# Loading the second half of w2 in even pieces instead of three uneven ones, and the first MLP bias in five transfers instead of two

## The chip, the cores and the metric

The kernel runs on one core of a Trainium2 chip. The metric is the device time of one execution in microseconds (us). The kernel before takes 134.59 us (median of 7 runs, 134.49 to 134.99).

## The reference

One decode step for two sequences (B = 2) with width D = 576. A layer norm of `x` feeds two branches whose sum is added to `x`. All inputs are bf16.

```python
xn = layernorm(x)                                    # 2 x 576
# branch A: attention over the last W = 2048 of 8192 cached positions
q = (xn @ wq)                                        # 32 query heads of 128, 16 key/value heads
p = softmax(q . k_cache[:, :, Sk - W:, :] * 128**-0.5)
a = (p . v_cache[:, :, Sk - W:, :]) @ wo             # 4096 -> 576
# branch B: MLP with squared ReLU
h = relu(xn @ w1 + b1) ** 2                          # 576 -> 4608
b = h @ w2 + b2                                      # 4608 -> 576
out = x + a + b
```

Nearly all the work is reading: 16 tiles of 2 MB of keys and values, and the weights wq (4.7 MB), w1 (5.3 MB), wo (4.7 MB) and w2 (5.3 MB); 53.6 MB in all, each byte used once.

## The kernel before, in words

**Tiling of the attention.** The key and value caches are cut into NU = 8 units (four heads of one sequence each). `load_k(u)` and `load_v(u)` (line 106) each issue one transfer of 2 MB, 128 rows of 16384 bytes, one row per partition. `step(u)` transposes the keys of unit u on TensorE, forms its scores and softmax, and in between does the value product of unit u - 2. `issue_flat` (line 119) loads wq, w1 and wo, in this order of time, into the one buffer `wbig`, each as one transfer; so w1 waits until wq has been read by the matmuls, and wo until w1 has.

**The queues.** All large loads are issued from the queue of SP, in the order of the program. The few small ones (x, the two rows of four of b1 at line 417, b2 at line 418, and the output) are issued from the queue of ACT. Every transfer, on either queue, has one of eight completion semaphores, which are handed out in turn; a transfer that gets a semaphore for a second time is issued only when the transfer that had it before has landed, unless an earlier wait of the same queue already showed that. The order of the hand-outs is that of the compiled program. In the kernel before it is: x, k0, b1 (first), b1 (second), b2, wq, k1, v0 on the eight semaphores; then k2 on that of x, v1 on that of k0, k3 on that of the first half of b1, v2 on that of the second, and so on. At the end, the three pieces of `w2x_sb` are on the semaphores of k7, v6 and v7, and the last piece of `w2c_sb` on that of wo.

**The end.** `out_ps` is one PSUM tile in which 128 columns of attention output (wo, 32 rows of four matmuls), the first half of the MLP (w2a, 18 rows) and its second half (18 rows) are added up by `out_acc`, four matmuls for each row of a partition. w2 is seen as two halves; in each a partition holds 18 consecutive rows of 576 values, 1152 bytes each. The first half is one transfer (`w2a_sb`, 20736 bytes per partition). The second half comes in pieces, in this order on the SP queue:

- `w2b_sb`: rows 0 to 8 of each partition (10368 bytes per partition)
- `w2c_sb`: rows 9 to 13 (5760 bytes), then rows 14 and 15 (2304 bytes)
- `w2x_sb`: row 17, in three transfers of 85, 25 and 18 partitions (`XS`, line 77; lines 442 to 444)
- `w2c_sb`: row 16 (1152 bytes)

The matmuls follow in the order of arrival (lines 451 to 457); row 17 (`w2x_sb`) is taken just before row 16, which is the last. ACT then copies `out_ps` to SBUF (line 460) and stores it (line 461).

Of the kernel before, what the change touches and what calls it, by code (L numbers as in the profile page):

```python
# [8 lines left out]
F32 = mybir.dt.float32  # L9
BF16 = mybir.dt.bfloat16  # L10
# [6 lines left out]
def kernel(  # L17
# [14 lines left out]
    nc = tc.nc  # L32
    P = 128
    B, Sq, D = A_x.shape
# [26 lines left out]
    NG4 = 4  # L61
# [11 lines left out]
    WC = Dh // WR  # L73
    FR = L1 // P
    assert HW == 32 * FR and QH * 2 == NC and NC * WC == 32
    W2P = [(0, 9), (9, 14), (14, 16), (16, 17)]
    XS = [(0, 85), (85, 110), (110, 128)]
    BS = 16
    MB = BS * (B - 1) + 1
    RM = 32 * (NG4 - 1) + MB  # L80
# [3 lines left out]
    const = ctx.enter_context(tc.tile_pool(name="const", bufs=1))  # L84
    kvpool = ctx.enter_context(tc.tile_pool(name="kvpool", bufs=6))
    wbig = ctx.enter_context(tc.tile_pool(name="wbig", bufs=1))
    w2pool = ctx.enter_context(tc.tile_pool(name="w2pool", bufs=1))
# [5 lines left out]
    def matmul(*a, **k):  # L93
        tc.keep_in_program_order(nc.tensor.matmul(*a, **k))  # L94
# [24 lines left out]
        nc.sync.dma_start(out=tl[:, 0:n], in_=w.rearrange("r n -> (r n)").rearrange("(p l) -> p l", p=P))  # L119
        return tl  # L120

    const.tile([P, 112], F32, name="pad_0")
    w2x_sb = const.tile([P, D], BF16, name="w2x_sb")
    xb_sb = const.tile([B + 1, D], BF16, name="xb_sb")
    x_sb = xb_sb[0:B, :]
    nc.scalar.dma_start(out=x_sb, in_=x2d)
# [54 lines left out]
    for t0, half, k0, n, pc in ((0, 0, 0, NK, 0), (0, 1, 0, NK, 1), (1, 0, 1, NK - 1, 1), (1, 1, 0, NK - 1, 0)):  # L181
# [11 lines left out]
                          in_=own[:].unsqueeze(2).to_broadcast([P, NC, WC]))  # L193
# [11 lines left out]
                          in_=ident[0:2 * NG4, 0:2 * NG4].rearrange("p (x g) -> p x g", g=NG4).unsqueeze(3)  # L205
                          .to_broadcast([2 * NG4, 2, NG4, B]))

    b1_sb = const.tile([2 * NG4, HW], BF16, name="b1_sb")
    w2_rows = B_w2.rearrange("(x p r) n -> x p (r n)", x=2, r=FR)


    out_ps = psum.tile([RM, OQ], F32, tag="out", name="out_ps")
    nc.vector.memset(out_ps[:], 0.0)

    def out_acc(lhsT, rhs, o, start=False, stop=False):
        for i in range(4):
            matmul(out_ps[32 * i:32 * i + MB, :], lhsT=lhsT, rhs=rhs[:, o * D + i * OQ:o * D + (i + 1) * OQ],
                   start=start, stop=stop, skip_group_check=True, tile_position=(0, 32 * i))
# [91 lines left out]
    hT_sb = const.tile([P, 2, FR, MB], BF16, name="hT_sb")  # L310
# [75 lines left out]
    def step(u):  # L386
        fin = None
        w = u - 2
        with_pv = w >= 0
        for g in range(NG):  # L390
            transposes(u, g)
            if with_pv and g == 1:
                pv(w, 0, 2)
            if with_pv and g == 2:
                pv(w, 1, 2)
                fin = pv_end(w)
            if g == TG + 1:
                scores(u, 0)
            if g == TG + 2 and fin:
                fin()  # L400
        scores(u, 1)
        softmax(u)
# [10 lines left out]
    softmax(0)  # L413
    load_v(2)
    b1_rows = B_b1.rearrange("(x n) -> x n", n=HW)
    for i in range(0, 2 * NG4, 4):
        nc.scalar.dma_start(out=b1_sb[i:i + 4, :], in_=b1_rows[i:i + 4, :])
    nc.scalar.dma_start(out=xb_sb[B:B + 1, :], in_=B_b2.rearrange("(o n) -> o n", o=1))
    step(1)
    load_k(4)  # L420
# [12 lines left out]
    mlp_h(w1_sb)  # L433
    wo_sb = issue_flat(A_wo, "wo")
    w2a_sb = w2pool.tile([P, FR * D], BF16, name="w2a")
    r9 = W2P[0][1]
    w2b_sb = kvpool.tile([P, r9 * D], BF16, tag="kv", name="w2b")
    w2c_sb = w2pool.tile([P, (FR - 1 - r9) * D], BF16, name="w2c")
    nc.sync.dma_start(out=w2a_sb[:], in_=w2_rows[0])
    nc.sync.dma_start(out=w2b_sb[:], in_=w2_rows[1, :, 0:r9 * D])  # L440
    for r0, r1 in W2P[1:]:
        if r1 == FR - 1:
            for p0, p1 in XS:
                nc.sync.dma_start(out=w2x_sb[p0:p1, :], in_=w2_rows[1, p0:p1, (FR - 1) * D:FR * D])
        nc.sync.dma_start(out=w2c_sb[:, (r0 - r9) * D:(r1 - r9) * D], in_=w2_rows[1, :, r0 * D:r1 * D])
    step(NU - 1)
    pv_all(NU - 2)
    pv_all(NU - 1)
# [1 line left out]
        out_acc(ws[:, r, :], wo_sb, r)  # L450
    for r in range(FR):
        out_acc(hT_sb[:, 0, r, :], w2a_sb, r)
    for r in range(FR - 1):
        if r == FR - 2:
            out_acc(hT_sb[:, 1, FR - 1, :], w2x_sb, 0)
        w, o = (w2b_sb, r) if r < r9 else (w2c_sb, r - r9)
        out_acc(hT_sb[:, 1, r, :], w, o, stop=(r == FR - 2))

    fin_sb = work.tile([RM, OQ], BF16, tag="fin", name="fin_sb")
    nc.scalar.copy(out=fin_sb[:], in_=out_ps[:])  # L460
# [31 lines left out]
```

## Time and profile before

| | |
|---|---|
| median of 7 runs | 134.59 us |
| the profiled execution's own time | 134.49 us |
| span of the profiled execution | 132.6 us |
| busy: TensorE / its weight loads / VectorE / ScalarE / GpSimd | 82.6 / 50.2 / 63.4 / 46.8 / 4.9 us |
| mean granted TensorE clock | 0.868 |
| moved from HBM | 53.62 MB, 404 GB/s over the span |
| SP queue's transfers (q1) | 3603 packets, 95.1% of what 16 engines could be busy in the span |
| instruction loads (q8) | 7 packets, 0.11 MB |

The span runs from the first to the last recorded instruction; the time holds 1.9 us more. A transfer is split over at most 16 DMA engines, and each piece of it that an engine moves is a packet. A transfer of 128 rows gives each engine eight packets and one more of 4 bytes, which adds to the completion semaphore. A figure such as "95.1%" is the time in which the packets ran, over 16 engines and the span. The trace has a start and a duration for each packet, but not the engine's name; on an engine with work queued, a packet starts 3 or 4 ns before the end of the one ahead of it, so that the packets can be put in 16 chains.

### The profile page before, as it was taken

How to read it: one execution, taken by the hardware profiler on the slowest of the kernel's cores; microseconds unless marked ns; L12 is line 12 of the kernel's file. 1: busy time of each engine (PE TensorE's matmuls, PEld its weight loads, DVE VectorE, ACT ScalarE, POOL GpSimd, SP SyncE). 2: the span in 40 equal slices, each digit the busy share in tenths (PEclk: the TensorE clock that was granted, in tenths of full speed). 3: DMA queues.
4: the chain of work that ended last, by engine and by line, in shares of the span. 5: the costliest groups of instructions: out<-in, count | busy, mean ns of one | idle time of the engine just before them, and what ended most of it. 6: DMA issues, size and time to landing. Idle time of an engine off the chain costs nothing.

```text
span 132.6 us, 2285 instructions
## 1 busy us (share of the span) xinstructions
PE 82.6 (62%) x949; PEld 50.2 (38%) x949; DVE 63.4 (48%) x176; ACT 46.8 (35%) x67; POOL 4.9 (4%) x15
## 2 busy tenths in 40 slices
PE   0079229599589687596595697204639973348451
PEld 0069102276344353353452553002346531137330
DVE  7754300245657587496586457420264477740000
ACT  5716400339476094373563445200206442000000
POOL 5000000010010100100100100100000001000000
PEclk9999986959999999999999689965775799756985
DMA  4999999999999999999999999989999999899960
GB/s 144 390 456 491 401 395 415 435 435 420 437 425 435 415 440 420 440 430 425 445 413 435 430 462 413 505 375 400 435 430 435 453 467 423 371 463 396 400 215 1
DMA packets 3646, 53.76 MB, mean 405 GB/s; under 512 B 426, under 2 KB 693, under 8 KB 949
## 3 DMA queue, kind: packets, MB, share of 16 engines
q1 hardware_dynamic: 3603, 53.61, 95.1%
q8 instruction: 7, 0.11, 0.3%
q10 hardware_dynamic: 34, 0.02, 0.0%
q14 instruction: 2, 0.02, 0.0%
HBM read 53.62 MB, written 0.00 MB: 404 GB/s over the span
## 4 chain that ended last, share of the span: by engine, by line
DMA 78%; PE 14%; SPq 2%; ACT 2%; DVE 1%; issue 1%; ACTq 0%; DVEq 0%
DMA w<-in_B_w_dram 25%; DMA w2c<-in_B_w_dram 24%; DMA k<-in_A_k_cache_dram 16%; DMA wq<-in_A_wq_dram 13%; PE kT_ps L97 4%; PE h_ps L94 3%; PE q_ps L94 3%; PE sc_ps L94 2%; PE out_ps L94 1%; SPq L106 1%; PE o_ps L94 1%; ACT kT L269 1%; DVE qrow L237 1%; ACT qrow L237 0%; DVE qz L253 0%
## 5 line engine op out<-in xcount | busy, mean ns | idle before, releaser
L97 PE MATMUL kT_ps<-ident_f,k 128*128 128x128 f32 x256 | 40.7, 307 | 7.4 <-DMA k<-in_A_k_cache_dram 6.1
L97 PEld LDWEIGHTS kT_ps<-ident_f,k 128*128 128x128 f32 x256 | 31.9, 157 | 21.7 <-issue 13.9
L269 ACT COPY kT<-kT_ps 128x1024 bf16<-128x1024 bf16 x32 | 31.9, 1012 | 19.8 <-PE kT_ps L97 19.7
L271 DVE COPY kT<-kT_ps 128x1024 bf16<-128x1024 bf16 x32 | 21.8, 681 | 6.2 <-PE kT_ps L97 5.8
L94 PE MATMUL sc_ps<-kT,qz 128*32 128x512 bf16 x128 | 10.4, 408 | 6.7 <-DVE kT L271 4.7
L301 ACT ACTIVATE p<-sc_ps,bias 128x512 bf16<-128x512 f32 x8 | 5.5, 687 | 21.4 <-DVE gown L297 21.3
L94 PE MATMUL o_ps<-v,pT 128*32 128x512 bf16 x128 | 11.0, 427 | 0.0
L94 PEld LDWEIGHTS <-xnT 128*4 128x4 bf16 x108 | 3.3, 113 | 16.1 <-issue 14.7
L304 DVE STREAM_TRANSPOSE pT<-p 128x512 bf16<-128x512 bf16 x8 | 5.7, 710 | 6.2 <-ACT p L301 6.2
L334 DVE SCALAR_TENSOR_TENSOR o<-o_ps,in_s,o 128x128 f32<-128x128 f32 x24 | 8.3, 345 | 0.4
L94 PE MATMUL h_ps<-w,xnT 128*4 128x288 bf16 x72 | 3.7, 388 | 7.5 <-DMA w<-in_B_w_dram 7.5
L290 DVE TENSOR_REDUCE m<-sc_ps 128x1 f32<-128x512 f32 x8 | 5.5, 692 | 5.3 <-PE sc_ps L94 5.3
L294 POOL PARTITION_ALL_REDUCE gmax<-m x8 | 2.9, 365 | 105.9 <-DVE m L292 105.9
L374 DVE TENSOR_TENSOR hrow<-t 100x1152 bf16<-100x1152 f32 x2 | 2.6, 1356 | 8.6 <-ACT t L372 8.6
L94 PE MATMUL q_ps<-wq,xnT 128*4 128x512 bf16 x36 | 3.7, 589 | 4.8 <-DMA wq<-in_A_wq_dram 4.8
L460 ACT CAST fin_sb<-out_ps 113x144 bf16<-113x144 f32 x1 | 0.3, 278 | 17.3 <-PE out_ps L94 17.3
L94 PE MATMUL op_ps<-o,of_h 128*32 128x129 f32 x16 | 3.4, 299 | 4.7 <-DVE o L334 4.7
L94 PEld LDWEIGHTS <-qz 128*32 128x32 bf16 x128 | 2.2, 97 | 10.5 <-DVE kT L271 7.2
L97 PE MATMUL pro_ps<-ident,xn_sb 2*128 2x2 bf16 x5 | 0.9, 181 | 6.8 <-DVE xn_sb L172 6.5
L332 DVE TENSOR_SCALAR o<-o_ps,in_s 128x128 f32<-128x128 f32 x8 | 2.8, 346 | 4.6 <-PE o_ps L94 4.5
L94 PEld LDWEIGHTS <-hT_sb 128*17 128x17 bf16 x144 | 2.7, 94 | 5.0 <-issue 4.8
L237 DVE CAST qrow<-q_ps 100x512 bf16<-100x512 f32 x1 | 0.7, 692 | 7.9 <-PE q_ps L94 7.9
(72 smaller groups left out, 57.6 us busy)
## 6 DMA issues: line engine op xcount, KB each, us to landing
k<-in_A_k_cache_dram SPq DMA_DIRECT2D x8, 2048.0 KB, 21.3
v<-in_A_v_cache_dram SPq DMA_DIRECT2D x8, 2048.0 KB, 26.5
w<-in_B_w_dram SPq DMA_DIRECT2D x1, 5184.0 KB
wq<-in_A_wq_dram SPq DMA_DIRECT2D x1, 4608.0 KB
wo<-in_A_wo_dram SPq DMA_DIRECT2D x1, 4608.0 KB, 21.6
w2a<-in_B_w_dram SPq DMA_DIRECT2D x1, 2592.0 KB
w2b<-in_B_w_dram SPq DMA_DIRECT2D x1, 1296.0 KB
w2c<-in_B_w_dram SPq DMA_DIRECT2D x1, 720.0 KB, 31.7
```

The lines of the kernel that those rows point to most:

```text
L94: tc.keep_in_program_order(nc.tensor.matmul(*a, **k))
L97: tc.keep_in_program_order(nc.tensor.transpose(*a, **k))
L237: cp(out=qrow[:, k * QW:(k + 1) * QW].rearrange("p (i a d) -> p i a d", a=2, d=Dh), in_=q_ps[0:RB, k * QW // 2:(k + 1) * QW // 2].rearrang ...
L269: nc.scalar.copy(out=kT, in_=kT_ps[:])
L271: nc.vector.tensor_copy(out=kT, in_=kT_ps[:])
L290: nc.vector.tensor_reduce(out=m1[:], in_=sc_ps[:], axis=AX.X, op=ALU.max)
L294: nc.gpsimd.partition_all_reduce(gmax[:], m2[:], channels=P, reduce_op=ReduceOp.max)
L301: nc.scalar.activation(out=p_sb[:], in_=sc_ps[:], func=ACT.Exp, bias=bias[:, 0:1], scale=scale, accum_out=o1[:, Dh:Dh + 1])
L304: nc.vector.transpose(out=pT[:].rearrange("p j r -> p (j r)"), in_=p_sb[:])
L332: nc.vector.tensor_scalar(scalar1=in_s[:, 0:1], scalar2=None, op0=ALU.mult, **kw)
L334: nc.vector.scalar_tensor_tensor(scalar=in_s[:, k:k + 1], in1=o1[:, 0:Dh], op0=ALU.mult, op1=ALU.add, **kw)
L374: nc.vector.tensor_tensor(out=h4[:, :, k * HB:(k + 1) * HB], in0=t4, in1=t4, op=ALU.mult)
```

## The change

The second half of w2 is 18 rows per partition on all 128 partitions throughout: `w2b_sb` is as it was (9 rows), and `w2c_sb`, now 9 rows wide, comes in pieces of 6, 2 and 1 rows. The tile `w2x_sb` and its three transfers are gone; row 17 is the last piece and the last row of matmuls, after rows 15 and 16. The tile `w2c_sb` is allocated earlier in the program, which changes its address, and a padding tile grows from 448 to 576 bytes, as 1152 bytes of `w2x_sb` leave the same pool. The eight rows of b1 come in five transfers of 2, 2, 2, 1 and 1 rows instead of two of 4 rows. There are as many transfers as before in all: three fewer on SP's queue and three more on ACT's. The semaphores are handed out in another order: x, k0, the first three of b1, wq, the last two of b1 on the eight; then b2 on that of x, k1 on that of k0, v0, k2 and v1 on those of the first three of b1, k3 on that of wq, v2 and k4 on those of the last two of b1. At the end, the last piece of `w2c_sb` is on the semaphore of k7.

```diff
-    W2P = [(0, 9), (9, 14), (14, 16), (16, 17)]
-    XS = [(0, 85), (85, 110), (110, 128)]
+    W2P = [(9, 15), (15, 17), (17, 18)]
+    R9 = 9
...
-    const.tile([P, 112], F32, name="pad_0")
-    w2x_sb = const.tile([P, D], BF16, name="w2x_sb")
+    const.tile([P, 144], F32, name="pad_0")
...
+    w2c_sb = w2pool.tile([P, (FR - R9) * D], BF16, name="w2c")
...
-    for i in range(0, 2 * NG4, 4):
-        nc.scalar.dma_start(out=b1_sb[i:i + 4, :], in_=b1_rows[i:i + 4, :])
+    for i0, i1 in ((0, 2), (2, 4), (4, 6), (6, 7), (7, 8)):
+        nc.scalar.dma_start(out=b1_sb[i0:i1, :], in_=b1_rows[i0:i1, :])
...
-    r9 = W2P[0][1]
-    w2b_sb = kvpool.tile([P, r9 * D], BF16, tag="kv", name="w2b")
-    w2c_sb = w2pool.tile([P, (FR - 1 - r9) * D], BF16, name="w2c")
+    w2b_sb = kvpool.tile([P, R9 * D], BF16, tag="kv", name="w2b")
     nc.sync.dma_start(out=w2a_sb[:], in_=w2_rows[0])
-    nc.sync.dma_start(out=w2b_sb[:], in_=w2_rows[1, :, 0:r9 * D])
-    for r0, r1 in W2P[1:]:
-        if r1 == FR - 1:
-            for p0, p1 in XS:
-                nc.sync.dma_start(out=w2x_sb[p0:p1, :], in_=w2_rows[1, p0:p1, (FR - 1) * D:FR * D])
-        nc.sync.dma_start(out=w2c_sb[:, (r0 - r9) * D:(r1 - r9) * D], in_=w2_rows[1, :, r0 * D:r1 * D])
+    nc.sync.dma_start(out=w2b_sb[:], in_=w2_rows[1, :, 0:R9 * D])
+    for r0, r1 in W2P:
+        nc.sync.dma_start(out=w2c_sb[:, (r0 - R9) * D:(r1 - R9) * D], in_=w2_rows[1, :, r0 * D:r1 * D])
...
-    for r in range(FR - 1):
-        if r == FR - 2:
-            out_acc(hT_sb[:, 1, FR - 1, :], w2x_sb, 0)
-        w, o = (w2b_sb, r) if r < r9 else (w2c_sb, r - r9)
-        out_acc(hT_sb[:, 1, r, :], w, o, stop=(r == FR - 2))
+    for r in range(FR):
+        w, o = (w2b_sb, r) if r < R9 else (w2c_sb, r - R9)
+        out_acc(hT_sb[:, 1, r, :], w, o, stop=(r == FR - 1))
```

## The prediction

> **What bounds the kernel now.** I read the strip of 40 slices first, then the DMA view, the chain that ended last, the waits of the SP queue, and the timeline of the last 5 us.
>
> ```profile
> DMA  4999999999999999999999999989999999899960
> GB/s 144 390 456 491 401 395 415 435 435 420 437 425 435 415 440 420 440 430 425 445 413 435 430 462 413 505 375 400 435 430 435 453 467 423 371 463 396 400 215 1
> DMA packets 3646, 53.76 MB, mean 405 GB/s; under 512 B 426, under 2 KB 693, under 8 KB 949
> q1 hardware_dynamic: 3603, 53.61, 95.1%
> q8 instruction: 7, 0.11, 0.3%
> ...
> DMA 78%; PE 14%; SPq 2%; ACT 2%; DVE 1%; issue 1%; ACTq 0%; DVEq 0%
> ```
>
> The DMA engines are full from the second slice to the 38th; every other engine is half idle. So a step counts only if it delays the stream, or lies after its end. The packet records are sharper: from 20 to 120 us every packet takes its minimum (16384 bytes in 611 ns, the next one 4 ns before its end), except the few that share an engine with an instruction load. The engines, not the memory, set the pace, and the stream ends when the last engine has done its own packets.
>
> ```profile
> 96.44 31.70 DMA w2c<-in_B_w_dram
> 128.15 0.04 issue
> 128.19 1.53 PE out_ps L94 x36
> 129.72 0.02 issue
> 129.74 0.28 ACT fin_sb L460
> ```
>
> ```profile
> 128.19 1.12 PE L94 MATMUL out_ps<-w2c,hT_sb 128*17 128x144 bf16 x28 [1.46 <-DMA w2c<-in_B_w_dram]
> ...
> 129.24 0.21 PEld L94 LDWEIGHTS <-hT_sb 128*17 128x17 bf16 x8 [0.24 <-DMA w2x_sb<-in_B_w_dram]
> 129.27 0.30 PE L94 MATMUL out_ps<-w2x_sb,hT_sb 128*17 128x144 bf16 x4
> 129.36 0.33 PE L94 MATMUL out_ps<-w2c,hT_sb 128*17 128x144 bf16 x4
> ```
>
> Here the reader sees the tail: matmuls follow the landings of w2's pieces. In the packet records w2a is complete at 122.45 and its first weights load at 122.84; w2b at 125.55 and 125.99; the second piece of w2c at 128.36 and 128.88; the last at 128.88 and 129.36. So a landing is 0.39 to 0.52 us ahead of its matmuls.
>
> **The engines in the tail.** Putting the packets in 16 chains gives three groups. Five engines carry all of row 17's first two transfers, 17 + 5 packets of 1152 bytes each, and 2 of the third; four carry 2 of the third; seven carry none. (The count agrees: 24 transfers of 16 completion packets and 5 + 5 + 9 are the 403 four-byte packets of q1.) Each engine is also hit by other things: six of the seven instruction loads fall on six different engines, none of the five, and each costs its engine 1.4 us (w2b done at 125.2 to 125.6 there, 123.7 to 124.2 on unhit ones). The seventh starts at 126.91, on an engine already done. Finishing times: the five at 127.93, 127.95, 128.13, 128.68 and 128.88; the six hit at 128.46 to 128.74; the other five at 126.7 to 127.0.
>
> **The change, part by part.**
>
> *Even pieces.* Packets follow each other every 216 ns (5760 bytes), 89 (2304), 47 (1152), 385 (10368); between 5760 and 10368 a packet of 6912 comes to 258. After w2b an engine now has 8 x 258 + 8 x 89 + 8 x 47 = 3152 ns. Before, the five had 8 x 216 + 8 x 89 + 8 x 47 + 24 x 47 = 3944, the four 2910, the seven 2816. So the five gain 0.79 us, the four lose 0.24, the seven lose 0.34. Of the hit engines one (done at 128.47) carried 2 packets of row 17, the others (128.46 to 128.74) none. They end at 128.71 and at 128.80 to 129.08; the five at 127.1 to 128.1; the unhit at 126.9 to 127.3. The stream ends at 129.08 instead of 128.88: +0.20 us.
>
> *A stall in the tail.* Between 126.4 and 128.25 almost all packets ran over their minimum (2304 bytes in up to 146 ns, for 93; 1152 in up to 105, for 51), on the latest hit engine 0.37 us in all. What causes it no row says. If it comes from row 17's uneven packets it goes with them, and the latest hit engine ends at 128.71, 0.17 us earlier than now. If it comes with small packets, worst case, the 6912-byte packets are stretched as the worst 5760-byte ones (305 ns for 220, so 0.36 of 258 for eight of them, 0.74 us instead of the 0.22 of that phase): +0.5 on the +0.20. I take it unchanged, as it slowed every group alike, and the engine that carries the end has the same small packets.
>
> *The matmuls of the tail.* Row 17's four matmuls and two waits between 129.17 and 129.36 go; six rows instead of five wait for the first piece. That piece lands 0.34 us later, at 127.82; its matmuls began 0.71 us after landing, so at 128.53 at the latest; six rows at 0.12 each (the pace of 128.33 to 128.57) end at 129.25. The second piece lands at 128.70, starts at 129.22, two rows, to 129.46. The last starts 0.48 after 129.08, at 129.56: still behind its transfer, by 0.1. Nothing is added. Were that cover gone, each row costs 0.12. The four matmuls, the copy to SBUF and the store after it are the same.
>
> *Five transfers of b1.* ACT issues three more (0.27 to 0.31 us each) between 4.4 and 6.2; its next instruction there, the square root at 5.63, feeds the transposes of xn, but q waits for wq until 18.7, so up to 12 us cover it. On the stream eight rows are the same bytes, with five rows on one engine and three on another instead of two on each of four: three packets of 51 + 9 ns, 0.18 us, on an engine that carried uneven packets before and ends at 128.1 at most after. Zero.
>
> *The semaphores.*
>
> ```profile
> 2.04 0.55 SPq L106 DMA_DIRECT2D k<-in_A_k_cache_dram  x1
> 2.62 0.71 SPq L106 DMA_DIRECT2D v<-in_A_v_cache_dram  x1
> 3.38 0.61 SPq L106 DMA_DIRECT2D k<-in_A_k_cache_dram  x1
> 8.33 0.53 SPq L106 DMA_DIRECT2D v<-in_A_v_cache_dram  x1
> 10.82 0.54 SPq L106 DMA_DIRECT2D k<-in_A_k_cache_dram  x1
> 14.42 0.54 SPq L106 DMA_DIRECT2D v<-in_A_v_cache_dram  x1
> ```
>
> k1, v0 and k2 were issued at 2.04, 2.62 and 3.38 and now wait: k1 for k0, as v1 did (8.33); v0 for the first of b1 (10.8, as k3 did); k2 and v1 for the second and third. Before, a row of b1 and its completion packet alternated with packets of wq, a row each 2.8 us (8.84, 11.62, 14.50); so the third lands near 15.9. k3 then waits for wq, 18.9, and v2 behind it, 19.5. Cover: wq keeps all engines busy to 18.5, and each 2 MB tile behind it for 4.9 us: k1 is wanted at 18.5, v0 at 23.4, k2 at 28.3, v1 at 33.2, k3 at 38.1, v2 at 43. Nothing runs dry by 9 us or more. From k4 on SP waits for transposes and value products as before (33.46 onward). At the end the last piece no longer waits for wo (issued 116.68) but for k7, so about 97.5; it lands at 128.88 behind w2b either way. Zero. b2 is wanted at 35.4 by its matmuls and lands near 21 behind five transfers of b1.
>
> *Addresses.* The move of `w2c_sb` and the padding changes no copy's shape; zero, with no row for it.
>
> **Sum.** +0.20 us on a span of 132.6, so 134.49 + 0.20 = 134.69 for an execution like the profiled one, which stands 0.10 under the median; on the median 134.79.
>
> **A rule against the trace.** The Trainium skill, page "DMA: Bandwidth & Descriptors", section "Why a DMA increments its semaphore by 16 and not by 1", says that a transfer runs on the largest number of engines up to 16 that divides its slowest dimension; 85, 25 and 18 partitions give 5, 5 and 9, which the chains here agree with. Its section "Rules for kernel authors" asks for all 16 engines and 128 partitions, which speaks for this change: were all engines equal at w2b, the five would set the end and the change would gain their 0.79 us. The trace differs, in that six other engines come 1.4 us late.
>
> **The rivals.**
>
> - *The stall was row 17's* (faster). For it: it starts at 126.39, soon after the first uneven packets (126.25), and stops at 128.25. Against: uneven packets run on unhindered to 128.4, and its width is near that of the last instruction load (126.91 to 128.06). It gives -0.17 us, 134.4; if the latencies to the matmuls shorten too, 134.3.
> - *The stall grows on the late engines* (slower). The worst row above: +0.7 us, 135.3; it decides from the point where the late engines' packets lose over 0.1 us more than now. For it: c1 packets on the hit engines were the first to be slow (126.39). Against: the number of engines active then is smaller.
> - *The stream runs dry early* (slower). If the waits for b1 were 9 us longer than read, each further us costs one; at 1 us, 135.8. Against: the landings at 10.3 and 13.1 above.
> - *It does nothing that counts*: the hit engines differ between executions, and both ends are equal: 134.6.
>
> **How the numbers follow.** Forecast 0.42, row 17's stall 0.22, growing stall 0.22, dry stream 0.04, nothing 0.10. 0.2% is 0.27 us, about what a measurement of this kernel can tell from no change. The forecast's own range is 134.55 to 135.0: +0.20 with 0.2 either way for the latencies of 0.39 to 0.52; a quarter of it is over the bound. Growing stall is over it in most of its range, the dry stream always. Row 17's stall gains more than 0.27 in about half. So faster 0.13, same 0.51, slower 0.36. The range leaves out the far part of the growing stall and the dry stream: 134.35 to 135.25.
>
> **What would show it.** Right: last packets of w2c at about 129.1 on engines hit by an instruction load, the five others a microsecond earlier; SP's k1 at 8.3 and k3 near 19 with a strip full of nines; the last matmuls at 129.5. Wrong: a gap in the strip before slice 10, a stall-free tail, a last piece waiting on TensorE, or an instruction load on an engine that is hit twice.

## The result and the profile after

| | before | after |
|---|---|---|
| median time | 134.58 us (38 runs) | 134.07 us (16 runs) |
| profiled execution: time / span | 134.49 / 132.6 us | 134.09 / 132.1 us |

The ratio is 0.9959, 95% interval 0.995 to 0.9968: 0.41% faster, half a microsecond. The forecast was 134.8 us, between 134.35 and 135.25, so the time lies outside the range and on the other side of no change.

The page of the kernel after, its strips (slices of 3.3 us) and its queues:

```profile
DMA  4999899999999999999999999999999999899960
GB/s 159 402 432 525 369 398 427 427 437 427 437 419 432 432 422 437 427 442 422 437 424 422 441 466 414 444 437 402 417 437 437 463 424 469 382 414 424 406 248 1
DMA packets 3499, 53.76 MB, mean 407 GB/s; under 512 B 407, under 2 KB 546, under 8 KB 802
q1 hardware_dynamic: 3456, 53.61, 95.1%
q8 instruction: 7, 0.11, 0.3%
```

The stream is as full as before and carries the same bytes, in 147 packets fewer on q1 (3456 against 3603). The gain is not in the middle. The chain that ended last shows the end (start, us, what):

```profile
97.91 31.03 DMA w2c<-in_B_w_dram
128.94 0.04 issue
128.98 0.27 PE out_ps L94 x4
129.25 0.02 issue
129.27 0.28 ACT fin_sb L454
```

Before, the copy to SBUF (the ACT line) began at 129.74, after 36 matmuls that had begun at 128.19; now the chain goes through the four matmuls of the last row alone. The timeline of the same microseconds (start, us, engine and instruction, in brackets the idle time before it):

```profile
127.94 1.28 PE L94 MATMUL out_ps<-w2c,hT_sb 128*17 128x144 bf16 x36 [1.35 <-DMA w2c<-in_B_w_dram]
127.94 0.40 PEld L94 LDWEIGHTS <-hT_sb 128*17 128x17 bf16 x24 [1.50 <-issue]
128.63 0.15 PEld L94 LDWEIGHTS <-hT_sb 128*17 128x17 bf16 x8 [0.28 <-issue]
128.98 0.09 PEld L94 LDWEIGHTS <-hT_sb 128*17 128x17 bf16 x3 [0.21 <-issue]
129.27 0.28 ACT L454 CAST fin_sb<-out_ps 113x144 bf16<-113x144 f32 x1 [17.44 <-PE out_ps L94]
```

The three groups of weight loads are the three pieces of 6, 2 and 1 rows; the last two start 0.25 and 0.38 us earlier than the work on the second and the last piece of `w2c_sb` before (128.88 and 129.36).

The view that tells most is the table of windows. For 126.2 to 128.2 us its columns are: stretch, length, busy time of the five engines, granted TensorE clock, DMA busy share, GB/s. Before:

```profile
126.20:128.20 2.00, 0.54 (x40) 0.39 (x28) 0.00 (x0) 0.00 (x0) 0.00 (x0) 1.00 0.82 270
```

After:

```profile
126.20:128.20 2.00, 0.65 (x44) 0.50 (x36) 0.00 (x0) 0.00 (x0) 0.00 (x0) 1.00 0.67 261
```

Before, the DMA engines were busy for 0.82 of the time and moved 270 GB/s, 329 GB/s for a full share; after, 0.67 and 261, so 390. Packets before took longer for their bytes. Some of that is the mix of sizes: had each packet that starts in the window run at the minimum of its size, before would have moved 379 GB/s for a full share and after 391 (worked out from the packet records). The rest is in the packets: after 126 us, 126 of the pieces' packets of before ran more than 5 ns over the minimum of their size; after, not one. The last instruction load falls in the same stretch in both profiles (126.91 to 128.06 before, 126.77 to 127.65 after), so it alone does not make the stall.

From this the half microsecond can be laid out. The first rows concern the latest engine that an instruction load had hit; times from the packet records, in us:

| | before | after | difference |
|---|---|---|---|
| that engine has done w2b | 125.55 | 125.39 | -0.16 |
| its packets after w2b, at the minimum | 2.82 | 3.15 | +0.33 |
| over the minimum | 0.37 | 0.03 | -0.34 |
| that engine done | 128.74 | 128.57 | -0.17 |
| last landing on any engine | 128.88 | 128.57 | -0.31 |
| last landing to the copy | 0.86 | 0.70 | -0.16 |
| copy to the end of the span | 2.86 | 2.85 | -0.01 |

The last three sum to -0.48, the difference of the spans (132.60 and 132.12). The first row need not be owed to the change: in two more profiles of the kernel after (e5_after_again and e10_after_third below) w2b was done at 125.46 and 125.58.

### The profile page after: what moved, and what is told of

The parts are those of the page before. It is cut to its first block, busy times and chain, and to the rows that moved or that the text cites. A ratio compares the mean times of both kernels' runs of the same rounds, so it can differ in the third digit from the quotient of the medians.

```text
span 132.1 us, 2284 instructions
## 1 busy us (share of the span) xinstructions
PE 83.2 (63%) x949; PEld 50.3 (38%) x949; DVE 63.0 (48%) x176; ACT 46.5 (35%) x67; POOL 4.9 (4%) x15
## 3 DMA queue, kind: packets, MB, share of 16 engines
q1 hardware_dynamic: 3456, 53.61, 95.1%
## 4 chain that ended last, share of the span: by engine, by line
DMA 77%; PE 16%; SPq 2%; DVE 1%; issue 1%; ACT 0%; ACTq 0%; DVEq 0%
DMA w<-in_B_w_dram 25%; DMA w2c<-in_B_w_dram 23%; DMA k<-in_A_k_cache_dram 15%; DMA wq<-in_A_wq_dram 13%; PE kT_ps L97 5%; PE h_ps L94 3%; PE q_ps L94 3%; PE sc_ps L94 2%; PE qT_ps L97 1%; SPq L106 1%; PE o_ps L94 1%; SPq L441 1%; DVE qrow L238 1%; DVE qz L254 0%; SPq L438 0%
## 5 line engine op out<-in xcount | busy, mean ns | idle before, releaser
L97 PE MATMUL kT_ps<-ident_f,k 128*128 128x128 f32 x256 | 39.6, 302 | 6.0 <-DMA k<-in_A_k_cache_dram 3.8
L97 PEld LDWEIGHTS kT_ps<-ident_f,k 128*128 128x128 f32 x256 | 31.2, 154 | 19.3 <-issue 10.7
L94 PE MATMUL h_ps<-w,xnT 128*4 128x288 bf16 x72 | 4.5, 442 | 8.7 <-DMA w<-in_B_w_dram 8.7
L94 PE MATMUL out_ps<-wo,ws 128*17 128x144 bf16 x128 | 4.0, 324 | 1.2 <-DVE ws L351 1.2
L373 ACT ACTIVATE t<-h_ps 100x288 f32<-100x288 f32 x2 | 0.7, 406 | 10.7 <-PE h_ps L94 10.7
```

The lines of the kernel that those rows point to most:

```text
L97: tc.keep_in_program_order(nc.tensor.transpose(*a, **k))
```

## The experiments

The theory after the result: row 17 was loaded mostly by five engines (110 of its 128 partitions) into partitions that other engines fill, and while all of them were writing, both sides were slowed. The rivals: the slowing comes from small packets or from the few engines as such, wherever they write; the five transfers of b1 give the gain; or the profiled pair differs by chance. In the readings, an overlong packet is one of w2's later pieces that runs more than 5 ns over its minimum after 126 us; "in all" is the time by which these packets together exceeded their minima. "Span" is the mean over the timed runs against the kernel before on the same chip, with a standard error of about 0.03 us.

### The two halves of the change, alone

`e1_even_w2` is the kernel after with the old loop for b1; `e2_five_b1` the kernel before with the new one.

```diff
# e1_even_w2, against after
-    for i0, i1 in ((0, 2), (2, 4), (4, 6), (6, 7), (7, 8)):
-        nc.scalar.dma_start(out=b1_sb[i0:i1, :], in_=b1_rows[i0:i1, :])
+    for i in range(0, 2 * NG4, 4):
+        nc.scalar.dma_start(out=b1_sb[i:i + 4, :], in_=b1_rows[i:i + 4, :])
```

```diff
# e2_five_b1, against before
-    for i in range(0, 2 * NG4, 4):
-        nc.scalar.dma_start(out=b1_sb[i:i + 4, :], in_=b1_rows[i:i + 4, :])
+    for i0, i1 in ((0, 2), (2, 4), (4, 6), (6, 7), (7, 8)):
+        nc.scalar.dma_start(out=b1_sb[i0:i1, :], in_=b1_rows[i0:i1, :])
```

> The change with b1 left in its two transfers: only w2 is loaded evenly, and k1, v0 and k2 are issued at 2 to 3.4 us again. Theory: the gain has two parts, a tail without overlong packets (the last transfer 0.31 us earlier in the changed kernel, 0.15 of it owed to the start) and a start in which the first tile lands 0.2 us earlier because SP issues nothing while it runs. Then this kernel keeps the tail only: packets at their minimum after 126 us, first tile landed at about 7.9 us, ratio 0.997 to 0.998. Rival (the start differed by chance, or b1 has no part): ratio 0.996 as the whole change, first tile at 7.7.

> The kernel before with b1 in five transfers and w2 as it was: k1 issued at about 8.1 us. Theory (the start counts by itself): ratio 0.9985 to 0.999, first tile landed at about 7.7 us instead of 7.96, tail packets overlong as before (about 3 us in all). Rival (no part in it): ratio 1.000, first tile at 7.96.

| | median | ratio, interval | span | overlong packets, in all | last landing |
|---|---|---|---|---|---|
| e1_even_w2 | 134.43 us | 0.9989, 0.9981 to 0.9998 | -0.11 us | 0 | 128.79 |
| e2_five_b1 | 134.69 us | 1.0008, 0.9998 to 1.0019 | +0.10 us | 117, 2.45 us | 128.74 |
| before | | | | 126, 2.86 us | 128.88 |

The window of e1_even_w2, and then that of e2_five_b1:

```profile
126.20:128.20 2.00, 0.72 (x48) 0.52 (x39) 0.00 (x0) 0.00 (x0) 0.00 (x0) 1.00 0.71 275
```

```profile
126.20:128.20 2.00, 0.60 (x41) 0.45 (x33) 0.00 (x0) 0.00 (x0) 0.00 (x0) 1.00 0.81 275
```

275 GB/s take 0.71 of the engines with the even pieces (387 for a full share) and 0.81 with row 17's own transfers (340). So the slowing follows row 17 and not b1. But neither half alone gives the gain: the even pieces give a quarter of the 0.42 us of span that the kernel after gains (0.24 us in a repeat; both below), b1 gives none. The ratio of e1 is outside both of its expected ranges. The theory that b1 speeds the start falls: the first tile of keys landed at 8.03 us in e1 and 8.05 in e2, against 7.96 before. Something in the even pieces was paid back, and b1 in five transfers must undo that.

### Is it the few engines, or where they write?

`e3_one_95` and `e4_own_ports` both replace row 17's three transfers by ones that load 95 of its 128 partitions' rows through five engines, 19 packets each. In e3 the rows go to partitions 0 to 94 in order, 19 neighbouring partitions for each engine if they are dealt out in order (the trace does not show the dealing). In e4 the rows go to five partitions only, one for each engine (0, 4, 8, 12 and 16), in two transfers and into other tiles. Row 17's product is left out in both.

```diff
# e3_one_95, against before
-    XS = [(0, 85), (85, 110), (110, 128)]
+    XS = [(0, 95)]
...
-        if r == FR - 2:
-            out_acc(hT_sb[:, 1, FR - 1, :], w2x_sb, 0)
```

```diff
# e4_own_ports, against before (the same product left out)
-    w2b_sb = kvpool.tile([P, r9 * D], BF16, tag="kv", name="w2b")
+    w2b_sb = kvpool.tile([P, UE], BF16, tag="kv", name="w2b")
+    w2y_sb = kvpool.tile([P, UE], BF16, tag="kv", name="w2y")
...
-            for p0, p1 in XS:
-                nc.sync.dma_start(out=w2x_sb[p0:p1, :], in_=w2_rows[1, p0:p1, (FR - 1) * D:FR * D])
+            for t, o, q0, q1 in ((w2y_sb, 0, 0, 70), (w2b_sb, r9, 70, 95)):
+                n = (q1 - q0) // 5
+                nc.sync.dma_start(out=t[0:17:4, o * D:(o + n) * D].rearrange("p (r n) -> p r n", n=D),
+                                  in_=w2_rows[1, q0:q1, (FR - 1) * D:FR * D].rearrange("(e r) n -> e r n", e=5))
```

> Row 17 of the second half is loaded for 95 partitions only, in one transfer that runs on five engines, 19 packets of 1152 bytes each; the product with row 17 is left out. Control for the next run. Theory (uneven packets slow the others): packets over their minimum by about 19/24 of the 3 us seen after 126 us before, so 2 to 3 us in all, and the engines hit by an instruction load 0.2 to 0.4 us longer in the tail than their minimum. Rival (the stall came from something else in that execution): no packet over its minimum.

> The same 95 rows of row 17 are read, again on five engines with 19 packets of 1152 bytes each (14 and 5), but they are written into five partitions only, 0, 4, 8, 12 and 16, one for each engine; the product with row 17 is left out. Theory A (an engine that writes into partitions which another engine also fills slows both): the stall goes, packets at their minimum after 126 us, 0 to 0.3 us over in all. Theory B (the extra small packets or their reads make the stall, wherever they are written): as in the control, 2 to 3 us over in all.

The queue and the window of e3_one_95:

```profile
q1 hardware_dynamic: 3556, 53.57, 95.0%
...
126.20:128.20 2.00, 0.74 (x47) 0.59 (x38) 0.00 (x0) 0.00 (x0) 0.00 (x0) 0.96 0.77 270
```

And of e4_own_ports:

```profile
q1 hardware_dynamic: 3561, 53.57, 95.1%
...
126.20:128.20 2.00, 0.97 (x56) 0.82 (x54) 0.00 (x0) 0.00 (x0) 0.00 (x0) 0.98 0.76 287
```

The same bytes go through the same number of packets, but for e4's extra transfer (five 4-byte packets). Yet e3 moves 351 GB/s for a full share and e4 378. The mix of sizes does not differ here: at their minima the packets of the window would give 382 in both. In the records, e3 has 66 overlong packets (1.51 us in all, under the 2 to 3 us expected), e4 none. The times, of one execution each, are 134.26 and 134.07 us (0.06 of the difference is the program's end, see below). So neither small packets nor five engines make the stall: where they write does. The partitions are what was changed on purpose; that e4 also writes into other tiles was not tested apart.

The Trainium skill, page "DMA: Bandwidth & Descriptors", section "The descriptor swizzle", gives the map from which e4's partitions were taken: in a transfer of 128 partitions each engine writes eight fixed partitions, four neighbours and the four 32 further on, and these share one port of SBUF; engine 0 has 0 to 3 and 32 to 35, engine 1 has 4 to 7 and 36 to 39, and so on. The trace has no engine names, so no run here shows the map itself; that writes along it lost nothing and writes across it lost 1.51 us agrees with it.

### Putting the crossing back into the kernel after

`e7_halves` loads the last piece, row 17, in two transfers of 64 partitions. Both use all 16 engines. The theory takes it that 64 partitions are dealt out to the engines in another way than 128; the trace does not name the engines, so the dealing itself is not seen.

```diff
# e7_halves, against after
-        nc.sync.dma_start(out=w2c_sb[:, (r0 - R9) * D:(r1 - R9) * D], in_=w2_rows[1, :, r0 * D:r1 * D])
+        for p0, p1 in ((0, P),) if r1 < FR else ((0, 64), (64, P)):
+            nc.sync.dma_start(out=w2c_sb[p0:p1, (r0 - R9) * D:(r1 - R9) * D], in_=w2_rows[1, p0:p1, r0 * D:r1 * D])
```

> The changed kernel with its last piece (row 17 of the second half, 128 partitions) in two transfers of 64 partitions each. Each engine still moves eight packets of 1152 bytes, with one completion packet more, but half of them may go to partitions that another engine fills. Theory (an engine that writes into another's partitions slows both): if the 64 partitions are dealt out four in a row, half of the packets cross and some 1152-byte packets run over their minimum at the end, 0.5 to 1.5 us over in all, last landing 0.05 to 0.2 us later. Rival (evenness alone matters), or the dealing respects the partitions' owners: none over its minimum, last landing within 0.03 us, time within 0.1 us of the changed kernel.

134.52 us, ratio 0.9994 (0.9977 to 1.001): splitting one piece of 144 KB, which changes no engine's bytes, gives back nearly all of the gain, 0.33 us against the kernel after on the same chip (134.19, below). The records have 22 overlong packets, 1.27 us in all; 0.96 of it falls on twelve of the 6912-byte packets, up to 408 ns for 262. These belong to engines still on the earlier piece, while others, ahead of them, write the halves. The expectation had put the stall on the 1152-byte packets; only two of the 22 are. The window moves 363 GB/s for a full share:

```profile
126.20:128.20 2.00, 0.52 (x36) 0.37 (x24) 0.00 (x0) 0.00 (x0) 0.00 (x0) 1.00 0.71 258
```

The last landing is at 128.89, against 128.57, 128.64 and 128.76 in the three profiles of the kernel after. The timeline shows what follows:

```profile
128.28 1.36 PE L94 MATMUL out_ps<-w2c,hT_sb 128*17 128x144 bf16 x36 [1.56 <-DMA w2c<-in_B_w_dram]
129.34 0.10 PEld L94 LDWEIGHTS <-hT_sb 128*17 128x17 bf16 x4 [0.21 <-DMA w2c<-in_B_w_dram]
129.69 0.28 ACT L455 CAST fin_sb<-out_ps 113x144 bf16<-113x144 f32 x1 [17.29 <-PE out_ps L94]
```

The first piece's matmuls begin at 128.28 instead of 127.94 (128.01 and 128.13 in the other two profiles): the piece that was not touched is late. Two steps more in the program's end (next part), about 0.11 us, are in the 0.33 too, which leaves some 0.22 us for the stall (an estimate).

### What the five transfers of b1 are for

In e1_even_w2 the copy began at 129.46, 0.28 us before that of the kernel before, but its span was only 0.1 us shorter (132.5 against 132.6). What is lost lies behind the copy. At the program's end SP waits for the eight DMA semaphores in a fixed order (line 481). The waits of the kernel after (us in total, times, longest):

```profile
SPq L481 <- DMA w2b<-in_B_w_dram: 27.5, 1, 27.5
...
SPq L481 <- DMA w2c<-in_B_w_dram: 3.0, 3, 2.0
SPq L481 <- DMA out_dram<-fin_sb: 2.3, 1, 2.3
```

And of e1_even_w2:

```profile
SPq L481 <- DMA w2c<-in_B_w_dram: 30.5, 1, 30.5
SPq L481 <- DMA out_dram<-fin_sb: 2.3, 1, 2.3
```

In the first the output is the last of five waits; in the second it is the second of two, and the semaphores behind it, whose transfers had long landed, are walked afterwards. The semaphore records of SP show the steps (us):

```
after:               131.307 output seen                                    131.372 next phase
e1_even_w2:          131.495 output seen  131.562  131.627  131.688         131.753 next phase
e9_b1_five_wo_four:  131.57  output seen  131.623  131.690  131.755  131.816  131.881 next phase
```

The output is seen 2.04 us after the copy's start; the next phase begins 2.10 us after it in the kernel after, 2.29 in e1: three more steps, 0.19 us. The semaphores are handed out in turn, so the place of the output hangs on the number of transfers: with 32, as before and after, it is the last of the walk, with 29, as in e1, three steps follow it, with 35, as in e2_five_b1, four (its next phase begins 2.35 us after the copy, 0.25 us more). To test this, `e8_b1_two_wo_four` brings e1 back to 32 transfers by loading wo in four pieces, and `e9_b1_five_wo_four` does the same to the kernel after, which makes 35 (the last row above; the moment at which its output is seen is the copy's start plus 2.04, as its record begins with the wait). The kernel after and e1 were run again beside them (`e5_after_again` and `e6_even_again` on one chip; `e10_after_third` with e8 and e9 on another).

```diff
# e8_b1_two_wo_four, against e1_even_w2; e9_b1_five_wo_four, against after
-    def issue_flat(w, name):
+    def issue_flat(w, name, parts=1):
...
-        nc.sync.dma_start(out=tl[:, 0:n], in_=w.rearrange("r n -> (r n)").rearrange("(p l) -> p l", p=P))
+        for i in range(parts):
+            c0, c1 = i * n // parts, (i + 1) * n // parts
+            nc.sync.dma_start(out=tl[:, c0:c1], in_=w.rearrange("r n -> (r n)").rearrange("(p l) -> p l", p=P)[:, c0:c1])
...
-    wo_sb = issue_flat(A_wo, "wo")
+    wo_sb = issue_flat(A_wo, "wo", 4)
```

> The changed kernel once more, beside a repeat of the run with even w2 alone. In the first profile its sixteen opening packets took about 0.7 us each, and about 0.95 us in the kernel before and in all four runs so far; every later landing is earlier by 0.2 to 0.3 us for it. Theory A (the opening belongs to the whole change, though neither part alone shows it): opening packets at 0.7 us again, ratio 0.995 to 0.997. Theory B (the opening belongs to the chip or to the placement in that job): opening packets at 0.95 us, ratio 0.9985 to 0.9995, as for even w2 alone.

> Even w2 with b1 in two transfers again, same chip as the run above. Theory A: opening packets at 0.95 us, ratio 0.998 to 0.9995, so 0.3 us slower than the changed kernel. Theory B: the same time as the changed kernel within 0.1 us.

> Even w2 with b1 in two transfers, but wo in four instead of one, so that there are 32 transfers again, as in the kernel before and the changed one, and the output has the last of the eight semaphores. Theory A (five transfers of b1 count only by keeping the number at 32: SP ends by walking through the semaphores in order, and with the output on an earlier one it has three more steps of 0.065 us behind its landing): the span as the changed kernel's within 0.07 us, one step behind the output, ratio 0.996 to 0.9975. Theory B (they count at the start, by k1, v0 and k2 being issued later): as even w2 alone, 0.15 us slower than the changed kernel, ratio 0.998 to 0.999.

> The changed kernel with wo in four transfers, 35 in all, the output on the third of the eight semaphores. Theory A: three more steps of SP behind the output's landing, span 0.15 to 0.25 us longer than the changed kernel's, ratio 0.998 to 0.999. Theory B: the span of the changed kernel within 0.07 us, ratio 0.996 to 0.9975.

> The changed kernel a third time, as the measure for the two runs above on the same chip: ratio 0.995 to 0.998, span 132.1 to 132.3, one step of SP behind the output's landing.

| | b1 / wo in | transfers | median | ratio, interval | span | last landing / copy |
|---|---|---|---|---|---|---|
| e5_after_again | 5 / 1 | 32 | 134.19 us | 0.9966, 0.9949 to 0.9982 | -0.42 us | 128.64 / 129.34 |
| e6_even_again | 2 / 1 | 29 | 134.31 us | 0.9979, 0.9962 to 0.9996 | -0.24 us | 128.55 / 129.30 |
| e8_b1_two_wo_four | 2 / 4 | 32 | 134.28 us | 0.9971, 0.9953 to 0.999 | -0.30 us | 128.99 / 129.60 |
| e9_b1_five_wo_four | 5 / 4 | 35 | 134.62 us | 0.9995, 0.9978 to 1.0012 | -0.02 us | 128.90 / 129.53 |
| e10_after_third | 5 / 1 | 32 | 134.18 us | 0.9954, 0.9937 to 0.997 | -0.42 us | 128.76 / 129.51 |

e6 begins its copy 0.04 us before e5 and ends its span 0.15 us behind it. With b1 in two, three transfers more make the kernel no slower (-0.24 to -0.30, a difference within the noise); with b1 in five, the same three make it slower (-0.42 to -0.02). It is the count that decides, and with it the walk. The profiles show it directly: from the copy to the end of the span the kernels with 32 transfers took 2.85 to 2.87 us, those with 29 took 3.03 and 3.05, those with 35 took 3.09. Not all came as expected: e8 lies 0.12 us of span behind e10, where 0.07 was allowed, and e9 0.40, where 0.15 to 0.25 was expected. The surplus goes with wo in four transfers, whose last landings are the latest of the table; why was not tested. In the waits of e9_b1_five_wo_four the output comes first of all (line 483):

```profile
SPq L483 <- DMA out_dram<-fin_sb: 22.6, 1, 22.6
```

In those of e8_b1_two_wo_four it is behind the pieces of w2 again:

```profile
SPq L483 <- DMA w2b<-in_B_w_dram: 17.1, 1, 17.1
...
SPq L483 <- DMA w2c<-in_B_w_dram: 3.0, 3, 2.0
SPq L483 <- DMA out_dram<-fin_sb: 2.3, 1, 2.3
```

The four spans can be put together (an estimate, from spans that are worth 0.03 us each, of two chips): the two kernels with 32 transfers sum to -0.72, the two with 29 and 35 to -0.26, so the steps of both cost 0.46 us, where the records say 0.19 + 0.25. Taking the records' values, the even pieces without the walk give -0.43 (e6), b1 in five +0.01 (e5), wo in four +0.13 (e8), and for e9 follows -0.04, measured -0.02. So b1's five transfers gain nothing by themselves. They replace the three transfers taken away from w2, and keep the output on the last semaphore.

One row does not fit: by these terms the span of e2_five_b1 should be 0.26 us longer than before; it was 0.10 longer. In its profile the longer walk is there in full, but its copy began 0.15 us earlier than before. On that chip e1_even_w2 too gained less than its repeat (-0.11 against -0.24). No run settles that.

## Why the prediction was wrong

**"A stall in the tail ... I take it unchanged."** This is the step that failed. The stall went entirely, as the first rival had it: 126 overlong packets to none, 0.37 us on the latest hit engine to 0.03. The reason given for keeping it, that it slowed every group of engines alike, was no reason: e3 against e4 shows that the destination of row 17's packets decides, for all of them, and e7 shows it the other way round. That engines without a packet of row 17 were slowed because their own partitions were being written by others is the reading that fits the map named above; it is not seen in a trace. The reason against the rival, that uneven packets ran on unhindered to 128.4, says little. The last eight packets of each of the five engines, 0.38 us, are row 16's, which go to all partitions evenly; by the finishing times in the prediction, row 17's own then end by 128.30 on four of the five and at 128.50 on the last (an estimate). So the stall stopped about when row 17 ran out. A stall-free tail was also among the prediction's own signs of being wrong. The price given for the stall's going was 128.71 for the last landing, on the profiled start; measured 128.57, of which 0.16 us is that engine's earlier start into the tail, which the prediction did not have and which varies between executions.

**Even pieces, +0.20 us.** The size of the term was right. A 6912-byte packet follows the one before in 258 ns as interpolated, and 3.15 us of packets after w2b is what the late engines took. The +0.34 for their added bytes came as said, and the stall's 0.37 paid for it; the 0.14 us by which the five uneven engines had outlasted the others was gained besides.

**The matmuls of the tail: nothing added.** Nothing was, but something was taken away. From the last landing to the copy the two profiles of uneven loading took 0.86 and 0.85 us; the kernel after and e1, e5, e6, e10 took 0.70, 0.67, 0.70, 0.75 and 0.75 (e8 and e9, with wo in four, 0.61 and 0.63). Row 17's four matmuls and its wait, just ahead of the last row, were costed as covered. e3 and e4, which load row 17 unevenly but leave them out, took 0.82 and 0.79, so they are worth 0.04 to 0.07 us; where the rest lies no run shows. Part of the 0.16 in the profiled pair is the clock. The windows of the last stretch, before and then after:

```profile
128.90:129.50 0.60, 0.60 (x19) 0.32 (x15) 0.00 (x0) 0.00 (x0) 0.00 (x0) 0.50 0.00 0
```

```profile
128.90:129.50 0.60, 0.27 (x8) 0.09 (x3) 0.00 (x0) 0.23 (x1) 0.00 (x0) 1.00 0.00 0
```

The granted clock was 0.50 there in before, e6 and e10, and 1.00 in after, e1 and e5. e2_five_b1 had 1.00 and still took 0.85, so the clock is not the whole of it; e3 and e4 had 0.50, like before. Among the even kernels with wo in one transfer, those at 1.00 were 0.05 to 0.08 shorter.

**Five transfers of b1, and the semaphores: zero.** Right for what was costed: k1 was issued at 8.09 (forecast 8.3), v0 at 10.64 (10.8), k3 at 19.10 (near 19), and the strip stays full:

```profile
8.09 0.54 SPq L106 DMA_DIRECT2D k<-in_A_k_cache_dram  x1
10.64 0.54 SPq L106 DMA_DIRECT2D v<-in_A_v_cache_dram  x1
13.41 0.54 SPq L106 DMA_DIRECT2D k<-in_A_k_cache_dram  x1
16.23 0.54 SPq L106 DMA_DIRECT2D v<-in_A_v_cache_dram  x1
19.10 0.53 SPq L106 DMA_DIRECT2D k<-in_A_k_cache_dram  x1
19.75 0.54 SPq L106 DMA_DIRECT2D v<-in_A_v_cache_dram  x1
```

k2, which was to wait for the second landing, went out at 13.41 and v1 at 16.23, where 15.9 was forecast. The term that was not on the list, where the output's semaphore stands in the walk at the end, is worth 0.19 us; it came to zero here only because the count of transfers stays at 32. A change of the pieces alone would have lost it, as e1 did.

**The rivals.** The growing stall did not come: the 6912-byte packets ran at their minimum. (Its price was also a little low: 305 ns for 220 is 0.39 over, not 0.36, so 0.80 us and not 0.74.) The stream did not run dry. "It does nothing that counts", at 134.6, missed by 0.5 us. "The stall was row 17's" had the mechanism and, at 134.3 to 134.4, a price 0.2 to 0.3 us short; the missing parts are the last landing's earlier start and the shorter way from landing to copy. Its chance of 0.22 was too low for a stall that began within 0.14 us of the first uneven packets.

**The rule.** It was weighed for the number of engines only: five engines with 24 packets more against six that come late. By that the change should lose 0.20 us. The advice of 128 partitions turned out right here. The prediction did not ask which partitions an engine writes, and that is where e3 and e4 differ.

**Still open.** About 0.1 us of the gain in the mean span (-0.42) is in none of the terms (-0.15 for the last landing, by the mean of before and e2_five_b1, 128.81, against 128.66 for the kernel after's three profiles; -0.14 from there to the copy; -0.01 behind it). And the opening differs: the first 16 packets took 936 ns on average before and 727 after, and k0 landed at 7.96 and 7.73; but e2_five_b1 had 984, e5_after_again 836 (between the two values expected of it) and e6_even_again 899, so it varies from one execution to the next, and b1 is not its cause. A layout of w2 that gives the late engines' partitions fewer rows was not tried.

## What to carry to other kernels

When all DMA engines are full, a transfer over fewer partitions need not simply move work from late engines to early ones: here it also slowed the packets of other transfers, and did not where e4 sent its rows to one partition for each engine. Judge it by the GB/s for a full DMA share in the window where it runs; 329 here, against 390 for the even pieces (12 of the 61 between them is the mix of packet sizes). And when transfers are added or removed, look at which wait of the program's last instructions comes last: a change of three transfers moved the end by 0.2 us here, about half of what the edit that was meant gained.

## What was not expected of the hardware

- Two sets of packets with equal sizes, counts and sources differ by 1.51 us of engine time and by 351 against 378 GB/s for a full share; what was changed between them is where they are written.
- Two transfers of 64 partitions instead of one of 128, 144 KB together, stretched the packets of another transfer from 262 to as much as 408 ns, and the kernel by 0.33 us, of which some 0.11 us is the walk of the next line.
- After the output is seen, each further step of SP's walk over the semaphores takes 0.06 to 0.07 us, even where the transfers landed long before; three cost 0.19 us.
